# Stores on SyncE's queue, the running state in fp32 beside its block-diagonal copy, and another order in the opening and in block 1

## The chip, the cores and the metric

The kernel runs on one NeuronCore of a Trainium2 chip. The core has five engines that work through their own instruction lists in order and meet only at semaphores: TensorE (PE) multiplies matrices, VectorE (DVE) works element by element, ScalarE (ACT) applies functions and copies, GpSimd (POOL) works element by element and issues DMAs that convert types, and SyncE (SP) issues DMAs. ScalarE can issue DMAs as well. The metric is the device time of one execution in microseconds. A profile of one execution gives the span from the first instruction to the last, and every instruction's place in it.

## The reference: what is computed

A retention layer without softmax, for a batch of 4, 8 heads, 768 steps and a head size of 64, and behind it a two-layer product with a leaky rectifier:

```python
gamma = 1.0 - 2.0 ** (-5.0 - np.arange(H))
for t in range(S):
    state = gamma * state + einsum('bhd,bhe->bhde', k[:, :, t], v[:, :, t])
    y[:, :, t] = scale * einsum('bhd,bhde->bhe', q[:, :, t], state)
x = y.transpose(0, 2, 1, 3).reshape(3072, 512)
h = x @ w_in                                   # 512 -> 2048
g = np.maximum(h, 0) + alpha * np.minimum(h, 0)
out = g @ w_out                                # 2048 -> 512, fp32
```

Inputs and output are fp32.

## The kernel before

**Tiling.** The 3072 steps are cut into 12 units of 256 steps (three per batch element), a unit into two chunks of 128. Two units make a block of 512 tokens; there are six blocks. Within a chunk the retention is a masked product of scores with v; from chunk to chunk a state of 64x64 per head is carried.

**One unit.** `load` (L114) brings q, k and v from SP's queue into four rotating buffers each. `rescale` (L142) multiplies q and k by their decay into the fp16 tile `kdq`, on VectorE or GpSimd; `cast_v` (L155) converts v. The transpose of `kdq` into `kq` is made on TensorE for units 0 to 3 (`turn_pe`, L167: four 128x128 transposes into a PSUM tile `trb`, then a copy by ScalarE), and by a DMA transpose on SP's queue for units 4 to 11 (`turn_dma`, L163). `score_mm` (L243) makes the scores of two of four head pairs, `masks` (L262) multiplies them on VectorE by the causal mask. `sum_mm` (L197) makes the sum of k times v of both chunks in PSUM; the last unit of a batch element needs only its first. `state` (L220) adds the carried state (`ss`, L234) and decays it (`tg`, L239). The result is written, per head pair, as two diagonal 64x64 quarters of a 128x128 fp16 tile whose other quarters were set to zero once; six such tiles rotate (`tgbuf`, L98). The next state reads its predecessor out of that tile. `out_mm` (L275) adds the product of q with the state and the product of the masked scores with v, and ScalarE copies the result as `xT` (L311), the transposed input of the block's first product.

**One block's products.** `ffn1` (L319) is a generator: for each of 16 groups of 128 features it makes four products of 128x128 with 128x512 tokens into one PSUM bank (`hps`, L326), then a rectifier on ScalarE (`hm`, L336) and a combination on VectorE (`gt`, L337). With `early=m` the first m groups are made in two halves of 256 tokens, the first halves ahead of the block's second unit. `ffn2` (L356) makes, for four sets of 128 tokens, 16 products with `w_out` (`ops`, L365); ScalarE evicts each set (`os`, L374, six buffers) and gives out its store from its own queue (L378). For block 0 `ffn2` is cut into four parts by features, so that it can begin before all of `w_out` is there. `tick(gen, m)` (L381) emits the next m products of a generator, so that attention work of later units can be put between them.

**What sets the order.** The kernel writes the order of every engine by hand: an engine and a DMA queue work in the order in which the program emits their instructions. Weights come by DMAs that GpSimd issues with conversion to fp16 (`get_wi`, `get_wo`, L389 and L393). `hold` (L103) makes the next load of a unit wait until a given weight piece has landed: the loads of unit 2 wait for the last piece of `w_in` (L448), those of unit 4 for the last piece of `w_out` (L498). PSUM has eight banks; each call is told which ones it uses, and waits until what was in them has been read.

**The stretches that the change touches.** The opening (L398 to L463) prepares units 0 and 1 and runs block 0's first product; `keep` (L91) issues products of a constant tile ahead of the work. L474 to L519 runs block 0's second product with units 2 and 3 between its pieces and begins block 1's first product. The loop at L522 runs blocks 1 to 5: in each, the next block's two units are rescaled on GpSimd and turned by DMA during the first product, and their attention is put between the pieces of the second product. All `state` calls of units 0 to 3 name VectorE; those in the loop name GpSimd for the decay, except the first of each batch element, which is always on VectorE.

Of the kernel before, what the change touches and what calls it, by code (L numbers as in the profile page):

```python
# [18 lines left out]
def kernel(  # L19
# [169 lines left out]
    def rows(x):  # L189
        return slice(64 * x, 64 * x + 64)  # L190
# [4 lines left out]
    sums = {}  # L195
# [24 lines left out]
    def state(u, c, eng):  # L220

        if (u, c) not in sums:
            return
        s = sums.pop((u, c))
        nxt = (u, 1) if c == 0 else (u + 1, 0)
        tg = tgbuf[(2 * u + c) % len(tgbuf)]
        tgs[nxt] = tg
        if u % UPB == 0 and c == 0:
            eng = nc.vector
        else:  # L230
            old = tgs[u, c]
            ss = sbp.tile([128, NP, 64], FP, tag="ss", bufs=3, name=f"ss{u}_{c}")
            for a in range(2):
                nc.vector.tensor_tensor(  # L234
                    out=ss[rows(a)], in0=old[rows(a), :, rows(a)], in1=s[rows(a)], op=ADD
                )
            s = ss
        for a in range(2):
            eng.tensor_tensor(  # L239
                out=tg[rows(a), :, rows(a)], in0=s[rows(a)], in1=dec[rows(a)], op=MULT  # L240
            )
# [33 lines left out]
    def out_mm(u, banks):  # L275
        _, kq, vx = prepped[u]
        ys = [ps(banks[0], "y0"), ps(banks[1], "y1")]
        inter = [(u, c) in tgs for c in range(2)]

# [75 lines left out]

    def ffn2(n, banks, parts=1):  # L356
        gt = gts.pop(n)
        opss = {}
        step = NFT // parts
        for f0 in range(0, NFT, step):  # L360
            for tq in range(4):
                if f0 == 0:
                    opss[tq] = ps(banks[tq % len(banks)], "ops")
                for ft in range(f0, f0 + step):
                    nc.tensor.matmul(  # L365
                        out=opss[tq],
                        lhsT=gt[:, ft, 128 * tq : 128 * tq + 128],
                        rhs=w_out_all[:, ft, :],
                        start=(ft == 0),
                        stop=(ft == NFT - 1),  # L370
                    )
                    if ft == NFT - 1:
                        os_sb = sbp.tile([128, d_model], FP, tag="os", bufs=6, name="os")
                        nc.scalar.activation(  # L374
                            out=os_sb, in_=opss[tq], func=COPY, bias=0.0, scale=1.0
                        )
                        row = TB * n + 128 * tq
                        nc.scalar.dma_start(out=out[row : row + 128, :], in_=os_sb)  # L378
                    yield
# [17 lines left out]

    nc.scalar.dma_start(out=tab, in_=tab_h.ap())  # L398
# [4 lines left out]
    nc.vector.memset(warm, 0.0)  # L403
    nc.vector.memset(spin, 1.0)  # L404
    nc.scalar.activation(out=warm, in_=warm, func=RELU, bias=0.0, scale=-1.0)
    for t in tgbuf:
        nc.vector.memset(t, 0.0)
    V, G, A = nc.vector, nc.gpsimd, nc.scalar
# [15 lines left out]
    nc.vector.tensor_scalar(  # L424
# [3 lines left out]
    keep(4)  # L428
# [3 lines left out]
    cast_v(A, 0, 4, 8)  # L432
# [4 lines left out]
    state(0, 0, V)  # L437
    turn_pe(1, 0, (2, 3))
    state(0, 1, V)
    out_mm(0, (4, 5))  # L440
    rescale(V, 1, 0, 4, 8)
    rescale(G, 1, 1, 4, 8)
    score_mm(1, 0, (6, 7))
# [12 lines left out]
    state(1, 0, V)  # L456
    state(1, 1, V)
# [8 lines left out]
    def early_prep(u, wos):  # L466
        rescale(V, u, 0, 0, 4)
        rescale(G, u, 1, 0, 4)
        rescale(V, u, 0, 4, 8)
        rescale(G, u, 1, 4, 8)  # L470
        cast_v(A, u)
        return get_wo(wos)

    gen = ffn2(0, (0, 1, 2, 3), parts=4)  # L474
    tick(gen, 18)
# [6 lines left out]
    tick(gen, 5)  # L482
    score_mm(2, 0, (6, 7))
    masks(2, 0)
    tick(gen, 3)
    turn_pe(2, 1, (4, 5))
    cast_v(A, 2)
    tick(gen, 6)
    score_mm(2, 1, (6, 7))
    masks(2, 1)  # L490
    sum_mm(2, (4, 5))
    state(2, 0, V)
    state(2, 1, V)
# [7 lines left out]
    tick(gen, 8)  # L501
    out_mm(2, (6, 7))
    turn_pe(3, 0, (4, 5))
    tick(gen, 5)
    score_mm(3, 0, (6, 7))
    masks(3, 0)
    tick(gen, 3)
    turn_pe(3, 1, (4, 5))
    cast_v(A, 3)
    tick(gen, 6)  # L510
    score_mm(3, 1, (6, 7))
    masks(3, 1)
    sum_mm(3, (4, 5))
    state(3, 0, V)
    state(3, 1, V)
    tick(gen)
    gen = ffn1(1, (0, 1, 2, 3, 4, 5), early=4)
    tick(gen, 16)
    out_mm(3, (6, 7))  # L519


    for n in range(1, NBLK):  # L522
# [4 lines left out]
        if more:  # L527
            for u in (u0, u0 + 1):
                tick(gen, 8 if n > 1 else 4)
                rescale(G, u, 0, 0, 8)  # L530
                rescale(G, u, 1, 0, 8)
                turn_dma(u)
                cast_v(G, u)
                if u + 2 < NU:
                    load(u + 2)
        tick(gen)
# [52 lines left out]
```

## Time and profile before

| What | Number |
|---|---|
| three executions | 232.33, 233.16, 234.44 us (median 233.16) |
| the profiled execution | 233.85 us, span 232.0 us |
| busy share of the span: PE, DVE, ACT, POOL | 89%, 55%, 43%, 29% |
| mean granted TensorE clock | 0.953 |
| TensorE busy, 58.45 to 73.30 us | 4.66 of 14.85 us, granted clock 0.66 |
| TensorE busy, 85 to 228 us | 141.90 of 143.00 us, granted clock 1.00 |
| DMA traffic | 34.01 MB, 147 GB/s on average |

The profile shows one execution. In its rows a group of instructions is named by line, engine, operation and tiles, written `out<-in`; behind it stand the number of instructions, their busy time, the mean of one, and the idle time ahead of them with what ended it. The 40 slices show each engine's busy tenths in equal parts of the span. The chain of work that ended last goes back from the last instruction to what released it, and so on. DMA issues show the time on the issuing queue, and apart from that the time from issue to landing. Releasers are inferred from the times of semaphore events.

### The profile page before, as it was taken

To read this page: it belongs to the slowest core of one execution; us is meant where nothing else is said; L and a number is where in the kernel's file an instruction comes from. 1 tells how busy PE (TensorE), PEld (TensorE's weight loads), DVE (VectorE), ACT (ScalarE), POOL (GpSimd) and SP (SyncE) were. 2 spreads that over 40 slices of the span, in tenths; PEclk is the share of its full clock that TensorE was granted. 3 is DMA by queue.
4 is the path that set the end of the run, shared out by engine and by line. 5 is a ranking of instruction groups with operands and counts; after the bars stand their busy time and mean duration, and the time that the engine had idled before them with its cause. 6 is when DMAs were issued, how large, how long until landed. Compare 5 with 4: busy or idle time off the path is not lost.

```text
span 232.0 us, 4867 instructions
## 1 busy us (share of the span) xinstructions
PE 207.5 (89%) x2045; PEld 105.7 (46%) x2045; DVE 128.7 (55%) x211; ACT 100.8 (43%) x168; POOL 67.4 (29%) x67
## 2 busy tenths in 40 slices
PE   7758899989317999999998999999999999999992
PEld 2436444545205545554453554455544555444440
DVE  4597588266400888602978406986068764288000
ACT  2553764534213672334842337723366323666121
POOL 0491015304920003891004970027900150000000
PEclk9985999999955899999999999999999999999998
DMA  6999999949999930269971199902660011100121
GB/s 186 293 185 196 202 286 276 187 89 271 271 247 270 247 87 3 91 144 285 214 175 48 49 237 283 284 15 91 137 138 0 3 45 72 67 0 0 48 86 53
DMA packets 62791, 34.01 MB, mean 147 GB/s; under 512 B 18080, under 2 KB 59696, under 8 KB 62768
## 3 DMA queue, kind: packets, MB, share of 16 engines
q1 hardware_dynamic: 54240, 23.07, 43.6%
q0 software_dynamic: 4752, 4.19, 11.9%
q10 hardware_dynamic: 3776, 6.43, 8.3%
q8 instruction: 16, 0.26, 0.5%
q14 instruction: 7, 0.06, 0.1%
HBM read 27.40 MB, written 6.29 MB: 145 GB/s over the span
## 4 chain that ended last, share of the span: by engine, by line
PE 80%; DMA 7%; DVE 6%; ACT 4%; issue 1%; POOL 1%; ACTq 0%; POOLq 0%
PE hps L326 37%; PE ops L365 31%; DMA kq<-kdq 4%; PE y L298 3%; DMA ks<-in_k_dram 3%; PE kps L94 3%; DVE m L266 2%; PE y L283 2%; DVE tg L239 1%; ACT xT L311 1%; PE sca L253 1%; PE st L208 1%; DVE ss L234 1%; ACT kq L181 1%; PE trb L175 1%
## 5 line engine op out<-in xcount | busy, mean ns | idle before, releaser
L337 DVE SCALAR_TENSOR_TENSOR gt<-hm,oma,hps 128x512 f16<-128x512 f32 x96 | 69.3, 745 | 58.1 <-ACT hm L336 51.1
L326 PE MATMUL hps<-xT,win 128*128 128x512 f16 (+1 forms) x408 | 88.2, 378 | 11.6 <-ACT os L374 8.8
L365 PE MATMUL ops<-wout,gt 128*128 128x512 f16 x384 | 87.3, 379 | 0.0
L336 ACT ACTIVATE hm<-hps 128x512 f32<-128x512 f32 x96 | 56.6, 597 | 27.2 <-PE hps L326 23.7
L326 PEld LDWEIGHTS <-win 128*128 128x128 f16 x408 | 41.2, 101 | 56.8 <-issue 12.6
L365 PEld LDWEIGHTS <-gt 128*128 128x128 f16 x384 | 36.1, 98 | 42.0
L374 ACT ACTIVATE os<-ops 128x512 f32<-128x512 f32 x24 | 14.3, 597 | 64.6 <-PE ops L365 53.4
L239 POOL TENSOR_TENSOR tg<-ss,tab 64x256 f16<-64x256 f32 x22 | 13.4, 610 | 82.4 <-DVE ss L234 81.5
L145 POOL TENSOR_TENSOR kdq<-qs,tab 128x512 f16<-128x512 f32 (+1 forms) x16 | 24.0, 1502 | 26.8 <-DMA qs<-in_q_dram 26.6
L266 DVE TENSOR_TENSOR m<-sca,mi 128x512 f16<-128x512 f32 x24 | 16.6, 690 | 19.8 <-PE scb L253 19.6
L311 ACT ACTIVATE xT<-y 128x512 f16<-128x512 f32 x24 | 16.0, 739 | 20.8 <-PE y L298 20.8
L145 POOL TENSOR_TENSOR kdq<-ks,tab 128x1024 f16<-128x1024 f32 x8 | 15.2, 1902 | 13.1 <-DMA ks<-in_k_dram 12.7
L266 DVE TENSOR_TENSOR m<-scb,mi 128x512 f16<-128x512 f32 x24 | 16.3, 681 | 0.0
L234 DVE TENSOR_TENSOR ss<-tg,st 64x256 f32<-64x256 f16 x32 | 13.3, 416 | 3.6 <-PE st L208 2.4
L181 ACT ACTIVATE kq<-trb 128x512 f16<-128x512 f16 x16 | 8.7, 597 | 12.5 <-PE trb L175 12.5
L253 PE MATMUL sca<-kq 64*64 64x128 f16 x192 | 8.5, 221 | 2.0 <-ACT kq L181 2.0
L283 PE MATMUL y<-kq,tg 128*128 128x128 f16 x80 | 7.5, 233 | 2.1 <-DVE tg L239 1.4
L253 PEld LDWEIGHTS <-kq 64*64 64x64 f16 x384 | 6.7, 108 | 4.6 <-ACT kq L181 3.0
L161 POOL CAST vx<-vs 128x1024 f16<-128x1024 f32 x8 | 8.5, 1061 | 0.7 <-DMA vs<-in_v_dram 0.7
L94 PE MATMUL kps<-spin 128*128 128x512 f16 x20 | 6.7, 490 | 2.2 <-DVE spin L404 1.5
L253 PE MATMUL scb<-kq 64*64 64x128 f16 x192 | 8.5, 222 | 0.0
L283 PEld LDWEIGHTS <-tg 128*128 128x128 f16 x80 | 5.8, 105 | 5.3 <-DVE tg L239 2.0
(25 smaller groups left out, 66.2 us busy)
## 6 DMA issues: line engine op xcount, KB each, us to landing
out_dram<-os ACTq DMA_DIRECT2D x24, 256.0 KB, 2.9
vs<-in_v_dram SPq DMA_DIRECT2D x10, 512.0 KB, 7.8
ks<-in_k_dram SPq DMA_DIRECT2D x8, 512.0 KB, 6.2
qs<-in_q_dram SPq DMA_DIRECT2D x8, 512.0 KB, 7.0
ks<-in_k_dram SPq DMA_DIRECT2D x8, 256.0 KB, 5.5
qs<-in_q_dram SPq DMA_DIRECT2D x8, 256.0 KB, 5.4
wout<-in_moe_w_out_dram POOLq DMA_DIRECT2D x4, 512.0 KB, 10.9
win<-in_moe_w_in_dram POOLq DMA_DIRECT2D x3, 512.0 KB, 9.5
```

What stands on the lines that cost most here:

```text
L145: eng.tensor_tensor(out=kdq[:, t, :, h0:h1, :].rearrange("p r h d -> p h r d"), in0=staged[u]["kq"[t]][:, h0:h1, :].rearrange("p h (r d) - ...
L234: nc.vector.tensor_tensor(out=ss[rows(a)], in0=old[rows(a), :, rows(a)], in1=s[rows(a)], op=ADD)
L239: eng.tensor_tensor(out=tg[rows(a), :, rows(a)], in0=s[rows(a)], in1=dec[rows(a)], op=MULT)
L253: nc.tensor.matmul(out=scs[a][rows(c), at : at + 128], lhsT=kv[rows(a), 0, r, p, rows(c)], rhs=qmove(kq, a, c, p), start=True, stop=True,)
L266: nc.vector.tensor_tensor(out=m2, in0=live[u, hh][a].rearrange("p (r a i) -> p r a i", r=2, a=2), in1=mask.unsqueeze(2).to_broadcast([128, ...
L283: nc.tensor.matmul(out=ys[c][:, 128 * p : 128 * p + 128], lhsT=tgs[u, c][:, p, :], rhs=kq.rearrange("p (t r a) i -> p t r a i", t=2, r=2)[ ...
L311: nc.scalar.activation(out=xT[n][:, :, at : at + 128].rearrange("k a (p r) -> k a r p", r=2), in_=ys[c].rearrange("k (a r p) -> k a r p", ...
L326: nc.tensor.matmul(out=hpss[ft][:, lo:hi], lhsT=w_in_all[:, hp, 128 * ft : 128 * ft + 128], rhs=xT[n][:, hp, lo:hi], start=(hp == 0), stop ...
L336: nc.scalar.activation(out=hm, in_=hps, func=RELU, bias=0.0, scale=-1.0)
L337: nc.vector.scalar_tensor_tensor(out=gt[:, ft, :], in0=hm, scalar=oma_sb[:, ft : ft + 1], in1=hps, op0=MULT, op1=ADD,)
L365: nc.tensor.matmul(out=opss[tq], lhsT=gt[:, ft, 128 * tq : 128 * tq + 128], rhs=w_out_all[:, ft, :], start=(ft == 0), stop=(ft == NFT - 1),)
L374: nc.scalar.activation(out=os_sb, in_=opss[tq], func=COPY, bias=0.0, scale=1.0)
```

## The change

*Stores.* The store of each evicted set is given out on SP's queue instead of ScalarE's.

*State.* The decayed state is made once as a plain fp32 tile (`tf`, 128x256, four buffers), from which the next state is added. VectorE adds over all 128 partitions in one instruction where it had two of 64 partitions. For the first state of a batch element VectorE multiplies; otherwise the engine that the call names does. Two GpSimd copies then put the quarters into the block-diagonal fp16 tile. All calls of units 0 to 3 now name GpSimd.

*Opening.* Three of the six zero fills go to GpSimd. The second `keep(4)` becomes `keep(3)`. Unit 1's turn and first scores come ahead of unit 0's `out_mm`, whose banks change; GpSimd's rescaling of unit 1 comes ahead of the states. The hold for unit 2's loads is put on the fourth of the five `w_in` pieces. Block 0's first product begins with four groups in halves, not two, with other banks.

*Block 0's second product, units 2 and 3.* The numbers of products between the attention steps change; unit 2's sums and state come ahead of its last masks; `cast_v(A, 3)` comes ahead of unit 3's turn. GpSimd's rescaling of units 4 and 5 and their DMA transposes are emitted here, unit 4's ahead of the last ten products of block 0, the transpose of unit 4 and the loads of unit 6 thus ahead of three of block 0's four stores.

*Block 1's first product* is made unit by unit: `ffn1_unit` makes all 16 feature groups for the 256 tokens of one unit, two groups to a bank. That of unit 2 stands between products of block 0's second, ahead of unit 3's attention. In the loop, block 1 starts with its second product.

The diff, cut to its core:

```diff
@@ state
+        t = sbp.tile([128, NP, 64], FP, tag="tf", bufs=4, name=f"tf{u}_{c}")
+        if u % UPB == 0 and c == 0:
+            nc.vector.tensor_tensor(out=t, in0=s, in1=dec, op=MULT)
+        else:
+            ss = sbp.tile([128, NP, 64], FP, tag="ss", bufs=3, name=f"ss{u}_{c}")
+            nc.vector.tensor_tensor(out=ss, in0=run.pop(), in1=s, op=ADD)
+            eng.tensor_tensor(out=t, in0=ss, in1=dec, op=MULT)
+        run[:] = [t]
...
         for a in range(2):
-            eng.tensor_tensor(
-                out=tg[rows(a), :, rows(a)], in0=s[rows(a)], in1=dec[rows(a)], op=MULT
-            )
+            o, i = tg[rows(a), :, rows(a)], t[rows(a)]
+            nc.gpsimd.tensor_copy(out=o, in_=i)
@@ new generator
+    def ffn1_unit(n, ul, banks):
+        if ul == 0:
+            gts[n] = sbp.tile([128, NFT, TB], F16, tag="gt", bufs=2, name=f"gt{n}")
+        gt = gts[n]
+        cols = slice(U * ul, U * ul + U)
+        for f0 in range(0, NFT, 2):
+            hps = ps(banks[f0 // 2 % len(banks)], "hps")
+            for f in range(2):
+                for hp in range(4):
+                    nc.tensor.matmul(
+                        out=hps[:, U * f : U * f + U],
+                        lhsT=w_in_all[:, hp, 128 * (f0 + f) : 128 * (f0 + f) + 128],
+                        rhs=xT[n][:, hp, cols],
+                        start=(hp == 0),
+                        stop=(hp == 3),
+                    )
...
+            hm = sbp.tile([128, TB], FP, tag="hm", bufs=3, name="hm")
+            nc.scalar.activation(out=hm, in_=hps, func=RELU, bias=0.0, scale=-1.0)
+            for f in range(2):
+                nc.vector.scalar_tensor_tensor(
+                    out=gt[:, f0 + f, cols], in0=hm[:, U * f : U * f + U],
...
@@ ffn2
-                        nc.scalar.dma_start(out=out[row : row + 128, :], in_=os_sb)
+                        nc.sync.dma_start(out=out[row : row + 128, :], in_=os_sb)
@@ opening
-    for t in tgbuf:
-        nc.vector.memset(t, 0.0)
+    for i, t in enumerate(tgbuf):
+        (G if i < 3 else V).memset(t, 0.0)
...
     cast_v(A, 0, 0, 4)
-    keep(4)
+    cast_v(A, 0, 4, 8)
+    keep(3)
...
     sum_mm(0, (0, 1))
-    state(0, 0, V)
+    rescale(G, 1, 1, 4, 8)
+    state(0, 0, G)
+    rescale(V, 1, 0, 4, 8)
     turn_pe(1, 0, (2, 3))
-    state(0, 1, V)
-    out_mm(0, (4, 5))
...
+    score_mm(1, 0, (4, 5))
     masks(1, 0)
-    turn_pe(1, 1, (0, 1))
+    turn_pe(1, 1, (2, 3))
     get_wi(4, 8)
-    get_wi(8, 12)
-    held.append(get_wi(12, 16))
+    out_mm(0, (6, 7))
+    state(0, 1, G)
+    score_mm(1, 1, (4, 5))
     cast_v(A, 1, 0, 4)
-    score_mm(1, 1, (4, 5))
     cast_v(A, 1, 4, 8)
     masks(1, 1)
+    held.append(get_wi(8, 12))
+    get_wi(12, 16)
     sum_mm(1, (2, 3))
...
-    gen = ffn1(0, (0, 1, 4, 5, 2, 3), early=2)
-    tick(gen, 8)
-    out_mm(1, (6, 7))
+    gen = ffn1(0, (6, 7, 0, 1, 2, 3), early=4)
+    tick(gen, 16)
+    state(1, 0, G)
+    out_mm(1, (4, 5))
+    state(1, 1, G)
     tick(gen)
@@ block 0's second product
     gen = ffn2(0, (0, 1, 2, 3), parts=4)
-    tick(gen, 18)
+    tick(gen, 10)
...
     score_mm(2, 1, (6, 7))
+    sum_mm(2, (4, 5))
+    state(2, 0, G)
     masks(2, 1)
-    sum_mm(2, (4, 5))
-    state(2, 0, V)
-    state(2, 1, V)
+    tick(gen, 7)
+    out_mm(2, (6, 7))
+    state(2, 1, G)
...
     held.append(get_wo(3))
     load(4)
     load(5)
-    tick(gen, 8)
-    out_mm(2, (6, 7))
+    tick(gen, 4)
+    half = ffn1_unit(1, 0, (4, 5, 6, 7))
+    tick(half)
+    cast_v(A, 3)
+    tick(gen, 3)
     turn_pe(3, 0, (4, 5))
...
     score_mm(3, 1, (6, 7))
+    sum_mm(3, (4, 5))
+    state(3, 0, G)
     masks(3, 1)
-    sum_mm(3, (4, 5))
-    state(3, 0, V)
-    state(3, 1, V)
+    tick(gen, 8)
+    out_mm(3, (6, 7))
+    state(3, 1, G)
+    rescale(G, 4, 0, 0, 8)
+    rescale(G, 4, 1, 0, 8)
+    cast_v(G, 4)
+    turn_dma(4)
+    load(6)
     tick(gen)
-    gen = ffn1(1, (0, 1, 2, 3, 4, 5), early=4)
-    tick(gen, 16)
-    out_mm(3, (6, 7))
+    half = ffn1_unit(1, 1, (4, 5, 0, 1, 6, 7))
+    tick(half, 20)
+    rescale(G, 5, 0, 0, 8)
+    rescale(G, 5, 1, 0, 8)
+    cast_v(G, 5)
+    turn_dma(5)
+    load(7)
+    tick(half)
```

More of the change, by code (lines that the diff above doesn't have):

```diff
@@ L423 @@
     )
-    nc.vector.tensor_scalar(
+    V.tensor_scalar(
         out=oma_sb, in0=aps[:, 0:NFT], scalar1=-1.0, scalar2=1.0, op0=MULT, op1=ADD
@@ L431 @@
     rescale(G, 1, 1, 0, 4)
-    cast_v(A, 0, 4, 8)
     masks(0, 1)
@@ L526 @@
             gen = ffn1(n, (4, 5, 6, 7, 0, 1))
[L527 to L536, printed above, removed]
+            if more:
+                for u in (u0, u0 + 1):
+                    tick(gen, 8)
+                    rescale(G, u, 0, 0, 8)
+                    rescale(G, u, 1, 0, 8)
+                    turn_dma(u)
+                    cast_v(G, u)
+                    if u + 2 < NU:
+                        load(u + 2)
+            tick(gen)
         gen = ffn2(n, (0, 1))
```

56 lines of the change are left out of this document (22 added, 34 removed).

## The prediction, made before the changed kernel ran

> **What bounds the kernel now.** I read the slices first, then the chain of work that ended last, then the timeline of the one stretch where both look odd, and last the waits. The slices:
>
> ```profile
> PE   7758899989317999999998999999999999999992
> PEclk9985999999955899999999999999999999999998
> DMA  6999999949999930269971199902660011100121
> ```
>
> One slice is 5.8 us. From slice 3 on TensorE is at 8 or 9 tenths, except in slices 10 and 11 (58 to 70 us), where it falls to 3 and 1 tenths; the clock is at half in slices 11 and 12. From 85 to 228 us it is busy 141.90 of 143.00 us: nothing is to be had there but by less TensorE work. The chain in order of time tells what fills the hole:
>
> ```profile
> 53.20 6.10 DMA ks<-in_k_dram
> 59.30 9.03 DMA kq<-kdq
> 68.37 0.04 issue
> 68.41 0.34 ACTq L378
> 68.75 0.05 issue
> 68.80 0.60 ACT os L374
> 69.40 0.04 issue
> 69.44 1.01 PE hps L326 x4
> ```
>
> A transpose on SP's queue ends at 68.33, and 0.08 us later ScalarE's queue gives out a store (L378), behind which the next eviction `os` and then TensorE's `hps` stand. The timeline shows that three of the four stores of block 0 do this:
>
> ```profile
> 58.89 0.36 ACTq L378 DMA_DIRECT2D out_dram<-os  x1
> 59.30 0.60 ACT L374 ACTIVATE os<-ops 128x512 f32<-128x512 f32 x1 [2.95 <-DMA vs<-in_v_dram]
> ...
> 62.51 0.34 ACTq L378 DMA_DIRECT2D out_dram<-os  x1
> 62.90 0.60 ACT L374 ACTIVATE os<-ops 128x512 f32<-128x512 f32 x1 [3.01 <-DMA qs<-in_q_dram]
> ...
> 68.41 0.34 ACTq L378 DMA_DIRECT2D out_dram<-os  x1
> 68.80 0.60 ACT L374 ACTIVATE os<-ops 128x512 f32<-128x512 f32 x1 [5.30 <-DMA kq<-kdq]
> ```
>
> Issue plus time to landing on SP's queue gives 58.8 (v of unit 4), 62.5 (q of unit 5) and 68.3 (transpose of unit 4); the stores go at 58.89, 62.51 and 68.41. So a store waits for an older transfer of the other queue, and ScalarE, which works in order, waits with it. The waits sum it up: `PE hps L326 <- ACT os L374` 8.8 us in 3 times, the longest 4.9. In 58.45 to 73.30, 14.85 us, TensorE is busy 4.66 at a mean clock of 0.66, and block 1's first product runs at half clock until about 76.
>
> **The change part by part.** I follow TensorE in absolute times of the profile.
>
> *Stores on SP.* The wait moves to SP's queue, which computes nothing. ScalarE is free, so the stretch above closes. What stands behind a waiting store on SP is transposes and loads; that is priced below. Issue time: 0.34 us on ACT, SP's own loads 0.37 to 2.6; I take 0.4, nearest to the store's own row. The last store's tail (228.2 to 232.0) stays, within 0.1.
>
> The Trainium skill, "DMA: Bandwidth & Descriptors", section "Issuing engines are not separate DMA queues", speaks against a gain: the issuing engine matters only by the little sequencer time. By it this part would be worth at most the 24 x 0.34 us of issue on ScalarE, all off the path; the 8.8 us wait above disagrees, since an in-order engine also inherits the wait ahead of the issue.
>
> *Opening (0 to 37.25).* One warm-up product fewer, 0.25 (L94, four in 1.02). Unit 1's turn and scores come ahead of unit 0's `out_mm`, which now waits for POOL: rescale ends at 14.6 (as before), two copies into `tg` follow, so `out_mm` starts at 15.4 instead of 13.48. POOL's copy 64x256 has no row; below lies a quarter of the 1.06 cast of 128x1024, 0.27, above the multiply of the same shape, 0.61; I take 0.4, nearest to the cast less a fixed part. The three memsets on POOL lie before q arrives at 5.5: nothing. ScalarE's casts of v1 come behind `xT`: 17.8 to 19.0 against 17.75 to 18.9, so `sum_mm(1)` ends at 19.4 to 20.1 (19.38 before). Then 16 half-width products instead of 8 (0.11 each at full clock, 0.23 at the half clock of 15.8 to 22.5): to 21.2 to 23.7. Meanwhile POOL issues weights (0.8 each, four after state (0,1)) until 20.9, then multiplies and copies state (1,0): 22.3. `out_mm(1)` thus ends at 23.3 to 24.9 (22.87 before), `xT` 1.33 later, and 16 halves (1.8) and 12 full features (10.35) remain: end at 36.8 to 38.3, I take 37.4 (before 37.25). Weights hide: the cast-loading queue is still moving older pieces until 18.2 and lands the last w_in piece at 26.9; the thirteenth feature is wanted at 34. Without that cover each late microsecond would cost one.
>
> *Start of block 0's second product.* Its first bank is now that of feature 14, not 12. Vector frees that bank 0.75 after the end of the first product (groups `gt`, 36.35 + 2 x 0.82 = 38.0): +0.8. So it begins at 38.2.
>
> *38.2 until `sum_mm(4)`.* Work: 71 products of 0.2155 = 15.3; block 1's first product unit by unit, 2 x 64 x 0.111 = 14.2 (eight halves took 0.86 from 24.29; as full products 13.8); units 2 and 3: turns 4 x 0.45, scores 4 x 0.35, sums 0.36 + 0.5, `out_mm` 1.03 + 0.85, together 6.0. Sum 35.5. The first product needs on DVE two 128x256 operations per pair; between 0.42 (64x256 rows of L234) and 0.745 (the 512-wide row), I take 0.42, of the same width: 0.84 against 0.89 on TensorE, hidden; at 0.745 it would cost 8 x 0.6 per unit, 9.6 in all. New waits: turn to scores takes 1.62 (41.13 to 42.75) and now has 4 and 5 products beside it, not 5 and 6: 0.3 + 0.1; `sum_mm(2)` for the cast 0.55 (0.25 before); `out_mm(2)` for masks behind the state add 0.25; the unit's product for `xT` 0.55; unit 3's scores 1.05, because ScalarE casts v3 (1.06) before it turns; small ones 0.2. Sum 3.0. So `sum_mm(4)` comes at 38.2 + 38.6 = 76.8, against 88.85: **-12.05**.
>
> *What is late next.* POOL does the states of unit 3 (DVE add at 65.1, POOL multiply 0.61, two copies) before it rescales unit 4: 67.1 to 70.9 (2 x 1.9), where before it followed the loads at 55.5. Block 0's weight piece and with it the loads of units 4 and 5 also come some 7 us later (POOL issues it at 49.7 behind state (2,0) and unit 3's rescaling, before at 42.04), landing by 72, about when POOL has used them up. Transpose 4 goes at 70.95 and lands in 4.7 to 6.2 (those of 99.43 and 132.33): 75.7 to 77.2, wanted at 77.5: hidden. Behind it on SP stand unit 6's loads (4.5, as 101.34 to 105.87) and three stores (1.2); rescaling unit 5 on POOL ends at 75.8, so the queue decides: transpose 5 goes at 78.7. Second transposes landed after 6.9 to 10.6; with loads ahead of it I take 9.2: 87.9 (85.6 to 89.3). `score_mm(5)` wants it 7.6 after `sum_mm(4)` (88.85 to 96.44), at 84.4. **+3.5**, between 1 and 5.
>
> *State in fp32, later blocks.* DVE adds once where it added twice (0.42 less each), POOL multiplies once and copies twice instead of multiplying twice: 1.4 for 1.22. The next add waits for the multiply alone. Only the units of block 3, with four states (118.8 to 137.1), have TensorE wait for them, 0.66 at 127.6 (it waits for the last add to free the sums' bank); the chain gets over 1 us shorter: **-0.66**. Stores ahead of transposes there: the queue is free for transpose 6 at 106.1 instead of 99.43, transpose 7 lands at about 121.3 and is wanted at 128.5: hidden by 7 us.
>
> Sum: 233.85 (span 232.0 and 1.85 around it) - 12.05 + 3.5 - 0.66 = 224.6. The profiled execution is 0.7 above the median of the three runs (233.16), so I forecast **224.0** for the median.
>
> **The rivals.** *Transpose 5 is in time* (its landing nearer 6.9, or POOL and SP quicker than I add): 220.5. For it: the term is the difference of two long chains; against: loads of unit 6 alone, without any store, keep the queue until 77.5, which with 7.8 to 8.9 to land is still past 84.4. *The clock falls in the wait for transpose 5.* After 3.0 us of idle (60.55 to 63.55) the granted clock fell to half at 63.66, and dense work from 73.29 got it back at 76.1. Here 2.8 us at half clock would lose 1.4, with a second such stretch 3: 225.5 to 227. The Trainium skill, "TensorE: Matmul & The Clock Gate", section "What's actually happening", puts the throttle after an idle window of about 3.4 us that runs freely, so whether a 3.5 us gap hits it is chance; the fall after 3.0 us fits no fixed count of idle time. *The change doesn't do what it says*: ScalarE still waits, for something else, and the 8.8 us stay in the sum: 233. Nothing in the new order has ScalarE wait for a transfer but the casts, whose loads are long in; little chance. *Slower: SP's queue holds up every block.* Place: blocks 2 and 3, where transposes stand behind the previous block's last store. Price: each landing later than the 7 us of slack costs its excess once per block; to outweigh 9.2 and a measurable 2.3 it takes 5.8 in both blocks, so a second transpose that lands 22 us after its issue. Against: none in the trace took over 10.6. Time 236.
>
> **How the numbers follow.** Forecast 0.44, clock 0.22, in time 0.20, no effect or an opening and vector pace at their bad ends 0.08, slower 0.06. The range reaches from in time with a good opening (219.5) to the clock's case with a bad opening, transpose 5 at 89.3 and some vector pace: 230.5. About 1% is what a measurement of this kernel tells from no change; below 230.8 is faster: 0.86, within 0.07, slower 0.07.
>
> **What would show it.** Right: no `ACT os <- DMA` waits and a hole in TensorE of 2 to 5 us only ahead of unit 5's scores, at 84 to 88, released by `kq<-kdq`; `sum_mm(4)` at 76 to 78; block 1's first product in two stretches of about 7.1 us each; POOL's rescaling of unit 4 at 66 to 68. Wrong if the 256-wide pieces are paced by DVE, if the opening's end leaves 36.8 to 38.3, or if idle time appears ahead of the scores of units 6 to 11.

## The result, and the profile after

The changed kernel takes 226.31 us (median of 225.29, 225.69, 226.94 and 227.53), the kernel before 233.69 in the four runs beside it: a ratio of 0.969 [0.962, 0.977]. The forecast was 224.0 with a range of 219.5 to 230.5. The profiled execution is the 225.29 one, with a span of 223.5 us against 232.0 before. The other three had spans of 223.9 to 225.8 at mean clocks of 0.966 to 0.977, where this one has 0.981; they left no profile, so the 1.0 between this execution and the median is not placed here. By an estimate from these clocks, 0.966 would fit two more stretches of 3.41 us at half clock (the length seen below; each lowers the mean of 225 us by 0.0076).

The slices of the changed kernel:

```profile
PE   7766798979899995999999999999999999999992
...
PEclk9998899999999999799999999999999999999998
DMA  6999999945696999939992169981190021100111
```

A slice is 5.6 us here. The hole of 3 and 1 tenths at 58 to 70 us is gone, and with it the half clock of slices 11 and 12. One weak slice is left, the sixteenth (83.8 to 89.4 us), and in the one behind it (to 95.0) the clock is at 7 tenths. The chain of work that ended last shows the place (start, duration, what):

```profile
75.96 1.51 PE ops L395 x7
77.47 0.56 PE st L208 x44
...
79.38 0.39 POOL tg L238
79.77 0.04 issue
79.81 0.24 POOL tg L238
80.06 7.23 DMA kq<-kdq
87.29 0.04 issue
87.33 0.24 PE sca L250
```

`sum_mm(4)` starts at 77.47. The transpose of unit 5 is issued at 80.06, lands at 87.29, and unit 5's scores go at once. The chain puts the issue of the transpose down to POOL's copy `tg`, which ended at 80.05. Releasers are inferred, and this one is a coincidence: SP's own queue shows what held the transpose.

```profile
71.45 2.90 SPq L165 DMA_TRANSPOSE kq<-kdq  x1
74.46 0.53 SPq L125 DMA_DIRECT2D ks<-in_k_dram  x1
75.05 0.57 SPq L125 DMA_DIRECT2D qs<-in_q_dram  x1
75.67 1.69 SPq L125 DMA_DIRECT2D vs<-in_v_dram  x1
77.45 2.50 SPq L408 DMA_DIRECT2D out_dram<-os  x3
80.06 5.20 SPq L165 DMA_TRANSPOSE kq<-kdq  x1
```

POOL has `kdq` of unit 5 ready at 76.1. Up to 80 us SP is at the loads of unit 6 and three stores. (The third experiment moves those loads: the transpose then goes at 77.38, before any such copy.) The waits (total, times, longest):

```profile
ACT os L404 <- PE ops L395: 59.7, 21, 6.8
...
PE sca L250 <- DMA kq<-kdq: 2.3, 1, 2.3
```

No wait of ScalarE for a transfer is in the list; before there were three ahead of `os`, of 3.0, 3.0 and 5.3, and one of 2.5 ahead of `hm`. What the new wait does to the clock is read from the windows; `PEclk` is the granted clock, behind the busy times of the engines:

```profile
core 0: us, PE busy (x) PEld busy (x) DVE busy (x) ACT busy (x) POOL busy (x), PEclk, DMA share, GB/s
77.47:85.00 7.53, 7.53 (x146) 4.29 (x145) 3.56 (x8) 1.20 (x2) 5.72 (x10) 1.00 1.21 290
85.00:97.80 12.80, 10.53 (x111) 5.08 (x106) 2.48 (x4) 3.26 (x5) 7.96 (x6) 0.87 0.79 216
97.80:219.00 121.20, 121.20 (x1095) 59.14 (x1094) 66.23 (x98) 55.81 (x92) 31.67 (x40) 1.00 0.45 114
...
88.68:92.09 3.41, 3.41 (x10) 1.22 (x8) 1.60 (x3) 0.00 (x0) 2.32 (x2) 0.50 1.21 297
```

From 88.68 to 92.09 us TensorE is busy without a gap at half the clock; just ahead of it and behind it the clock is 1.00. From unit 5's first scores to block 2's first product it takes 10.47 us (87.33 to 97.80) where before it took 8.58 (96.44 to 105.02): 1.89 more for the same work. Half of 3.41, 1.71, is the clock; the rest is about the 0.17 by which the scores before began ahead of the end of unit 4's `out_mm` (96.27), while here they begin behind a gap.

The whole difference of the spans can be put together from marks of the two traces:

| Stretch | Before | After | Difference |
|---|---|---|---|
| start to `sum_mm(4)` | 88.85 | 77.47 | -11.38 |
| `sum_mm(4)` to unit 5's scores | 7.59 | 9.86 | +2.27 |
| unit 5's scores to block 2's first product | 8.58 | 10.47 | +1.89 |
| block 2's first product to block 3's | 32.13 | 31.29 | -0.84 |
| from there to the last `os` | 90.44 | 90.44 | 0 |
| last `os` to the end | 4.41 | 3.97 | -0.44 |
| span | 232.0 | 223.5 | -8.5 |

### The profile page after: what moved, and what is told of

Its sections match the earlier page's. It is cut to its first block, busy times and chain, and to the rows that moved or that the text cites. A ratio compares the mean times of both kernels' runs of the same rounds, so it can differ in the third digit from the quotient of the medians.

```text
span 223.5 us, 5019 instructions
## 1 busy us (share of the span) xinstructions
PE 205.9 (92%) x2100; PEld 109.7 (49%) x2100; DVE 117.5 (53%) x194; ACT 101.2 (45%) x168; POOL 81.5 (36%) x104
## 4 chain that ended last, share of the span: by engine, by line
PE 80%; DMA 6%; ACT 5%; POOL 4%; SPq 2%; issue 1%; DVE 1%; DVEq 0%; ACTq 0%; POOLq 0%
PE ops L395 34%; PE hps L324 31%; PE hps L364 6%; DMA kq<-kdq 3%; PE y L296 3%; DMA qs<-in_q_dram 2%; PE y L281 2%; SPq L125 2%; PE st L208 2%; ACT xT L309 2%; ACT kq L181 1%; PE sca L250 1%; ACT vx L159 1%; POOL kdq L145 1%; POOL tg L238 1%
## 5 line engine op out<-in xcount | busy, mean ns | idle before, releaser
L395 PE MATMUL ops<-wout,gt 128*128 128x512 f16 x384 | 89.5, 385 | 0.6 <-DVE gt L335 0.6
L335 DVE SCALAR_TENSOR_TENSOR gt<-hm,oma,hps 128x512 f16<-128x512 f32 x80 | 59.3, 747 | 43.4 <-ACT hm L334 35.5
L324 PE MATMUL hps<-xT,win 128*128 128x512 f16 (+1 forms) x336 | 71.1, 373 | 1.4 <-ACT xT L309 1.4
L324 PEld LDWEIGHTS <-win 128*128 128x128 f16 x336 | 33.3, 99 | 37.9 <-issue 1.4
L238 POOL CAST tg<-tf 64x256 f16<-64x256 f32 x40 | 16.2, 405 | 35.7 <-DVE tf L228 33.8
L232 POOL TENSOR_TENSOR tf<-ss,tab 128x256 f32<-128x256 f32 x16 | 9.8, 610 | 42.3 <-DVE ss L231 41.5
L376 DVE SCALAR_TENSOR_TENSOR gt<-hm,oma,hps 128x256 f16<-128x256 f32 x32 | 14.0, 478 | 8.3 <-ACT hm L374 8.2
L364 PE MATMUL hps<-xT,win 128*128 128x256 f16 x128 | 14.3, 273 | 0.4 <-ACT xT L309 0.4
L181 ACT ACTIVATE kq<-trb 128x512 f16<-128x512 f16 x16 | 8.8, 595 | 12.2 <-PE trb L175 12.2
L364 PEld LDWEIGHTS <-win 128*128 128x128 f16 x128 | 12.5, 98 | 2.5 <-issue 0.7
L231 DVE TENSOR_TENSOR ss<-tf,st 128x256 f32<-128x256 f32 x16 | 6.6, 415 | 8.3 <-PE st L208 5.7
```

The costliest lines, as they stand in the source:

```text
L238: nc.gpsimd.tensor_copy(out=o, in_=i)
L324: nc.tensor.matmul(out=hpss[ft][:, lo:hi], lhsT=w_in_all[:, hp, 128 * ft : 128 * ft + 128], rhs=xT[n][:, hp, lo:hi], start=(hp == 0), stop ...
L335: nc.vector.scalar_tensor_tensor(out=gt[:, ft, :], in0=hm, scalar=oma_sb[:, ft : ft + 1], in1=hps, op0=MULT, op1=ADD,)
L364: nc.tensor.matmul(out=hps[:, U * f : U * f + U], lhsT=w_in_all[:, hp, 128 * (f0 + f) : 128 * (f0 + f) + 128], rhs=xT[n][:, hp, cols], sta ...
L376: nc.vector.scalar_tensor_tensor(out=gt[:, f0 + f, cols], in0=hm[:, U * f : U * f + U], scalar=oma_sb[:, f0 + f : f0 + f + 1], in1=hps[:, ...
L395: nc.tensor.matmul(out=opss[tq], lhsT=gt[:, ft, 128 * tq : 128 * tq + 128], rhs=w_out_all[:, ft, :], start=(ft == 0), stop=(ft == NFT - 1),)
```

## The experiments

The theory going in: the time is won by the stores leaving ScalarE's queue; the new order wins next to nothing and loses some 4 us to a late transpose 5 and the clock. The rival: the new order has the gain, or shares in it, and the stores' queue alone would only move the wait. "Before" in the ratios is the kernel before, on the same chip; brackets hold 95% intervals. The medians of the kernel before lie between 232.8 and 233.7 from one such comparison to the next, so a difference of medians between two experiments is uncertain by up to 0.9 us.

**1. The stores alone.** The kernel before, one line changed:

```diff
-                        nc.scalar.dma_start(out=out[row : row + 128, :], in_=os_sb)
+                        nc.sync.dma_start(out=out[row : row + 128, :], in_=os_sb)
```

> The kernel before with one edit: stores on SP's queue. Theory (the hole at 58 to 73 us is ScalarE waiting behind stores, and only the queue of the stores matters for it): no wait of ScalarE for a DMA, block 1's first product runs on from 58.5, unit 4's sums begin at 76 to 77 (88.85 before), transpose 5 lands long ahead of 84, span 219 to 221, so faster than the changed kernel (223.5). Rival (the hole is filled by the new order, with unit 2's part of block 1's first product put into it): TensorE still idles after 58 us for loads, transposes or copies, span 229 or more.

Measured: 221.65 us, ratio 0.953 [0.948, 0.959], 4.7 us less than the whole change (3.8 by the two ratios). SP's queue of this kernel:

```profile
54.40 2.71 SPq L125 DMA_DIRECT2D vs<-in_v_dram  x1
57.21 3.44 SPq L378 DMA_DIRECT2D out_dram<-os  x4
60.75 4.12 SPq L165 DMA_TRANSPOSE kq<-kdq  x1
...
67.93 4.97 SPq L165 DMA_TRANSPOSE kq<-kdq  x1
```

The four stores now cost SP 3.44 us ahead of transpose 4, and nobody waits for it: both transposes are issued long before `sum_mm(4)`, at 77.13, and no wait of ScalarE or TensorE for a transfer is left. From `sum_mm(4)` on this trace has the old distances (16.17 to block 2's first product, then 32.13). Before minus this kernel is 12.2 us of span: 11.7 ahead of `sum_mm(4)`, 0.4 in the tail. The Trainium skill, "DMA: Bandwidth & Descriptors", section "Issuing engines are not separate DMA queues", has the choice of issuing engine save only the usually small time on its sequencer; here it is 12.2 us for 24 x 0.34 us of issue, because the engine that issues also waits ahead of the issue.

What it waits for, the traces name: the semaphore on which each transfer reports its landing. In the kernel before, the queues of SP and ScalarE share eight of these, and a transfer is held until the one that last used its semaphore has landed. The stores of 58.89, 62.51 and 68.41 have the semaphores of unit 4's v, unit 5's q and unit 4's transpose, which land at 58.81, 62.44 and 68.33. In the kernel of this experiment SP's transfers, the stores among them, take the eight in turn behind the opening, and no store finds its semaphore in use: that of the first, at 57.21, had been free since 41.34. So the wait hasn't moved to SP's queue, it is gone. Whether stores on ScalarE's queue with other semaphores would do as well was not tried.

**2. The new order without the stores.** The changed kernel, the stores back on ScalarE's queue (the line above, the other way).

> The changed kernel with the stores back on ScalarE's queue. Theory (in the new order the transfers that block 0's stores wait for have landed before the sets are evicted at 66 to 70, and on SP the three stores only delay transpose 5): ScalarE waits for no DMA by more than 1 us, transpose 5 goes at 77.5 instead of 80.06 and lands by 85, the wait ahead of unit 5's scores is under 0.5 us (2.3 in the changed kernel), the clock stays up, span 219 to 221. Rival (the stores' queue carries the gain in either order): waits of ScalarE for loads and transposes come back with 3 us or more, span 227 or more.

Measured: 225.13 us, ratio 0.967 [0.962, 0.971]: not what was expected, 219 to 221, though not dearer than the changed kernel. Transpose 5 goes earlier without the stores ahead of it (76.53), but it lands only 0.83 earlier, at 86.46, and TensorE still waits 1.5: in every trace of this case SP's transfers land in the order of their issue, and unit 6's v, ahead of it, lands at 83.79. And ScalarE's waits are back, at another place, as its timeline shows at the end of block 1:

```profile
95.32 0.60 ACT L404 ACTIVATE os<-ops 128x512 f32<-128x512 f32 x1 [0.93 <-PE ops L395]
99.22 0.34 ACTq L408 DMA_DIRECT2D out_dram<-os  x1
99.67 2.73 ACT L334 ACTIVATE hm<-hps 128x512 f32<-128x512 f32 x5 [3.75 <-PE hps L324]
```

The store is given out at 99.22, 3.30 after its `os` ended. SP's load of k for unit 8, on the same semaphore, was issued at 92.28 and took 6.86 to land: 99.14. Five rectifiers `hm` then run in one burst and TensorE waits for what follows. The same happens at 131.35. So in the new order block 0's stores are not held up, but those of blocks 1 and 2 are: where such a wait falls depends on which transfer used the store's semaphore last. With the stores on SP's queue no store waits for a landing, neither in the order before (the first experiment) nor in the new one (the changed kernel). The change without the stores wins 8 us against the kernel before, the stores without the rest 11: both take the same hole away (`sum_mm(4)` comes at 77.29 here, at 77.13 in the first), so the two don't add up.

**3. Unit 6's loads behind transpose 5.** The changed kernel, one call moved:

```diff
     turn_dma(4)
-    load(6)
     tick(gen)
...
     turn_dma(5)
+    load(6)
     load(7)
```

> The changed kernel with unit 6's loads emitted behind transpose 5 on SP instead of ahead of it. Theory (the 2.3 us wait at 85 to 87.3 and the half clock at 88.7 to 92.9 both come from transpose 5 going late on a full queue): transpose 5 goes at 76.2, when GpSimd is through, lands by 82, no wait at 85, clock 1.00 to the end, span 219 to 220. Rival (transpose 5 is bound by GpSimd and by its own 7 us, or unit 6's loads turn late in its place): at most 1 us is gained, or the wait comes back at transpose 6 and 7; span 222 or more.

Measured: 221.98 us, ratio 0.953 [0.948, 0.957]. SP's queue:

```profile
72.49 3.20 SPq L165 DMA_TRANSPOSE kq<-kdq  x1
75.78 1.50 SPq L408 DMA_DIRECT2D out_dram<-os  x3
77.38 3.11 SPq L165 DMA_TRANSPOSE kq<-kdq  x1
80.58 0.53 SPq L125 DMA_DIRECT2D ks<-in_k_dram  x1
```

The transpose is issued 2.68 earlier, TensorE doesn't wait for it, and the clock is 1.00 from the opening on. That is 4.3 us less than the changed kernel by the medians, against the 2.27 + 1.89 = 4.16 of the table (the spans of the two profiled executions differ by 3.1, and this one began block 0's second product 1.02 later, which makes 4.1): the late transpose and the clock behind it are the whole loss, and moving unit 6's loads out of its way is enough to end it. The three stores still stand ahead of it here.

**4. Block 1's first product in one piece.** The changed kernel, `ffn1(1, ...)` behind unit 3's `out_mm` in place of the two calls of `ffn1_unit`:

```diff
-    half = ffn1_unit(1, 0, (4, 5, 6, 7))
-    tick(half)
...
-    half = ffn1_unit(1, 1, (4, 5, 0, 1, 6, 7))
+    half = ffn1(1, (4, 5, 0, 1, 6, 7))
```

> The changed kernel with block 1's first product made over 512 tokens in one piece behind unit 3's out_mm, instead of unit by unit. Theory (the piece ahead of unit 3 pushes GpSimd's rescaling of units 4 and 5 back by 7 us, and the 256-wide products cost 0.3 us more): GpSimd rescales unit 4 at 61 to 63, transpose 5 lands by 83, no wait for it, span 219.5 to 221. Rival (the piece ahead of unit 3 covers copies and masks that TensorE would wait for): the gain at transpose 5 is paid back by waits between 50 and 66 us, span 223 or more.

Measured: 222.55 us, ratio 0.956 [0.950, 0.961]. From block 0's second product to `sum_mm(4)` it is 38.99 us (38.95 to 77.94), in the changed kernel 38.92: making the product unit by unit neither wins nor loses time by itself. Transpose 4 is issued at 67.99 here and transpose 5 at 77.54, in time, though unit 6's loads stand ahead of it as in the changed kernel: GpSimd begins to rescale unit 4 at 61.66, 6 us earlier than there, as was expected. So the late transpose 5 needs both, the late rescaling behind the piece ahead of unit 3 and the loads in the queue; taking either away ends it.

**5. The new order with the old state.** The changed kernel, `state` as before (two additions from the fp16 tile, two multiplies into it, on the engine that the call names).

> The changed kernel with the state of before: two 64-row adds that read the fp16 block-diagonal tile, and the decay written straight into it. Theory (the fp32 state is worth what the four-state chain of units 6 and 7 made TensorE wait, 0.66 to 0.84 us, and one VectorE add of 0.42 in each of two spots of block 0): the wait of 0.7 ahead of unit 6's out_mm comes back, unit 2's and unit 3's steps each lose up to 0.4, the rest is as in the changed kernel; span 224.3 to 225.3 (223.5 in the changed kernel). Rival (the extra GpSimd copies cost as much as the add saves, since GpSimd's chain up to transpose 5 gets shorter without them): transpose 5 goes earlier by 0.4 or more, span 223.5 or less.

Measured: 228.29 us, ratio 0.979 [0.972, 0.985], above what was expected. Two of its waits:

```profile
PE sca L253 <- DMA kq<-kdq: 3.5, 1, 3.5
...
PE y L284 <- DVE ss L234: 0.7, 1, 0.7
```

The stretch of units 6 and 7 is 32.14 us again (31.29 in the changed kernel), with the wait for `ss` that the kernel before has too: the state in fp32 is worth 0.85 there. The rest of this execution's loss is transpose 5: it was issued at 79.88, about as in the changed kernel, and took 8.41 to land instead of 7.23, which makes the wait 3.5 instead of 2.3. The half clock follows in both, here from 88.82 to 92.23. Whether the old state has a part in the longer landing isn't shown. Nor is the median explained: the profiled execution, at 227.05, is the fastest of the four and had no half clock in its opening.

**6. Transpose 5 first, and other banks.** The third kernel, and block 0's second product begins with banks 2 and 3, whose features are read earlier:

```diff
-    gen = ffn2(0, (0, 1, 2, 3), parts=4)
+    gen = ffn2(0, (2, 3, 0, 1), parts=4)
```

> Unit 6's loads behind transpose 5, as in the run before, and besides block 0's second product on banks 2, 3, 0, 1 instead of 0 to 3, so that its first sets do not take the banks of the last two feature groups. Theory (the 1.3 us between the end of the first and the start of the second product is the bank, read last by VectorE): the second product follows the first within 0.1 us; the next thing late is VectorE's rescaling of unit 2 ahead of its transposes, some 0.5 us; net gain 0.8, span 218.3 to 219.7 with a usual opening. Rival (that wait only hides the later one for unit 2's rescaling or for its loads): the same start of unit 2's transposes as in the run before, no gain, the wait moves there.

Measured: 221.79 us, ratio 0.951 [0.946, 0.956], no different from the third's 221.98. The piece itself behaves: the wait of 0.60 ahead of `ops` is gone (the first product's rest takes 27.27 to 39.54, 12.27, where it was 12.87 with the wait), and from the start of that stretch to the end this execution is 0.66 shorter. But that stretch began at 27.27 instead of 26.70, and the total doesn't tell the two apart.

**7. The stores alone, and the fp32 state for block 3's units onward.** The first kernel, with the changed `state` from unit 6 on:

```diff
+        if u >= 2 * UPB:
+            t = sbp.tile([128, NP, 64], FP, tag="tf", bufs=4, name=f"tf{u}_{c}")
...
+            return
```

> The kernel before with stores on SP's queue and the fp32 state from unit 6 on only; opening, order and state of units 0 to 5 as before. Theory (of the new state only the four-state chain of units 6 and 7 is on the path): 0.8 us less than with the stores alone, span 218.6 to 219.4. Rival (that wait is hidden behind something else by then): span 219.8 as with the stores alone.

Measured: **220.58 us**, ratio 0.946 [0.941, 0.952], the least of all that was run, and faster than both kernels. The stretch of units 6 and 7 takes 31.29 (93.06 to 124.35) against 32.13 in the first: -0.84, and the medians differ by 1.07. The two parts that pay are thus the stores (or, by the second experiment, the new order in their place) and the fp32 state where TensorE waits for a chain of four states.

**8. The clock by itself.** The changed kernel, with ten products of the constant tile ahead of unit 5's scores; their result is read by nobody:

```diff
+            if n == 1:
+                keep(10)
             score_mm(u0 + 1, 0, (4, 5))
```

> The changed kernel with ten constant products (2.2 us at full clock, results unused) put in front of unit 5's scores, where TensorE waits for transpose 5. Theory (the wait itself costs 2.3 us and the half clock that follows it, 88.7 to 92.9, another 1.9): transpose 5 lands as before at 87.3, the wait behind the ten products is under 0.5 us, the clock stays at 1.00 from 85 to 95, span 221.4 to 222.0. Rival (the clock falls for another reason, or the products push the scores back by as much): half clock again, or scores after 88.5; span 223 or more.

Measured: 224.98 us, ratio 0.964 [0.959, 0.970], 1.3 less than the changed kernel though its profiled execution left the opening 0.93 later. Its windows, to be compared with the same one of the changed kernel above (0.87):

```profile
85.00:97.80 12.80, 12.32 (x157) 6.39 (x155) 2.48 (x4) 4.12 (x7) 8.90 (x6) 1.00 0.90 221
```

Transpose 5 lands as late as before (80.97 + 7.72 = 88.69), but from unit 5's scores to block 2's first product it now takes 8.77 us (88.74 to 97.51) instead of 10.47. So 1.70 of the 1.89 is the clock, and that is half of the 3.41 us; filling the gap with useless products gets it back, and only an earlier transpose gets the 2.27. The scores lie behind the rival's 88.5, but not because of the products, which end at 88.26: 0.93 is the later opening and 0.49 the longer landing.

**9. The new opening with the old middle.** The seventh kernel, with the fp32 state for all units and the opening of the changed kernel. Its core:

```diff
-    state(1, 0, V)
-    state(1, 1, V)
...
-    gen = ffn1(0, (0, 1, 4, 5, 2, 3), early=2)
-    tick(gen, 8)
-    out_mm(1, (6, 7))
+    gen = ffn1(0, (6, 7, 0, 1, 2, 3), early=4)
+    tick(gen, 16)
+    state(1, 0, G)
+    out_mm(1, (4, 5))
+    state(1, 1, G)
```

> Stores on SP's queue, the fp32 state in all units and the new opening, but units 2 and 3 and block 1's first product in the order of before. Theory (the new opening ends later: GpSimd's copies ahead of out_mm, twice as many half-width products ahead of unit 1's out_mm, and the bank of the second product): the second product begins 0.8 to 1.4 us later than with the old opening (37.4 to 38.2 in the three profiles with it), span 219.6 to 220.6 against 218.8. Rival (the later starts seen with the new opening, 38.4 to 39.6, are only where the clock's half-speed stretch falls): the start lies within 37.4 to 38.2 plus the bank's 0.7, span 219.3 or less.

Measured: 224.94 us, ratio 0.966 [0.962, 0.970]: 4.4 dearer than the seventh, and well above the 219.6 to 220.6 expected. The chain of this trace shows a wait that no other kernel has at this size:

```profile
50.50 0.76 POOL tg L238
51.26 0.08 issue
51.34 1.99 POOL kdq L145 x2
53.33 5.71 DMA wout<-in_moe_w_out_dram
59.05 0.04 issue
59.09 1.46 PE ops L362 x6
```

POOL issues the last piece of `w_out` behind its copies of unit 2's state, which are new there, and unit 3's rescaling: at 53.33, where the kernel before issued it at 42.04. TensorE waits 2.83 us for it. Of the 4.3 by which this span is longer than the seventh's, another 0.77 is a wait for POOL's copies of unit 2's state (1.09 ahead of `out_mm(2)`, against 0.32 for VectorE's there), and 0.77 the opening (the second product starts at 38.71, there at 37.94). In the changed kernel the piece is issued almost as late (50.98), but the products of `ffn1_unit` (51.03 to 58.18) stand ahead of its use. In the fourth, which has no such products there, 0.3 us of the same wait shows. The state's copies on POOL and the unit's product in the middle belong together: one makes the weight late, the other covers it.

**10. The new middle with the old opening.** The third kernel with the opening before, and with the old state for units 0 to 2.

> The opening of before (with its state in units 0 to 2), and behind it the changed kernel with unit 6's loads behind transpose 5. Against the stores alone with the fp32 state late (span 218.8) it differs in the order of units 2 and 3 and of block 1's first product alone. Theory (that order costs TensorE nothing and gains nothing once transpose 5 goes in time, since its waits are only exchanged): span 218.6 to 219.6. Rival (the unit-by-unit product is worth its 2 us of filled waits, hidden so far by the opening): span 218.3 or less.

Measured: 220.78 us, ratio 0.949 [0.943, 0.955]. From the start of block 0's second product to `sum_mm(4)` 38.57 (38.94 in the seventh; 38.93 in the third, which has the same order here), no wait for transpose 5. It equals the seventh kernel (220.58) within the spread of both: with transpose 5 in time, the new order of units 2 to 5 is worth nothing that these runs can tell, over the old one with its stores on SP.

**What the openings say.** Block 0's second product begins, over the profiled executions:

| Opening | Start of the second product, us |
|---|---|
| before's order (before; 1, 7, 10) | 37.41; 38.19, 37.94, 38.90 |
| new order (after; 2, 3, 4, 8, 9) | 38.55; 38.37, 39.57, 38.95, 39.48, 38.71 |
| new order, old state (5) | 38.05 |
| new order, other banks (6) | 39.54 |

Means of 38.1 and 38.9 for the first two rows: the new opening is no gain, and by this rather a loss of 0.8, 0.6 of it the wait for the bank. But one order varies by 1.5 between executions. They differ in the half clock of the first 26 us: it lasts 6.83 us in the four of the first row and in 2, 3, 4 and 8, but 3.41 in the changed kernel and 9, none in 5 and 10.24 in 6. The four of the second row with 6.83 have a mean of 39.1, so like with like the loss is 1.0; one execution of each kernel doesn't settle more.

## Why the prediction came out as it did

The time lies in the range, 2.3 above the forecast, and what was named as signs of being right is there: no wait of `os` for a transfer, a hole of 2 to 5 us only ahead of unit 5's scores, `sum_mm(4)` between 76 and 78, two stretches of about 7.1, unit 4's rescaling between 66 and 68. That the sum's 224.6 comes so near the profiled execution's 225.29 is in part luck: hole, transpose, clock, state and tail miss by +0.67, -1.23, +1.89, -0.18 and -0.44, and these cancel to +0.7. And the 0.6 taken off for the median went the wrong way, since the median lies 1.0 above the profiled execution. By the sum's own terms:

- **The hole closes: right.** -12.05 was forecast, -11.38 measured. `sum_mm(4)` was to come at 76.8 and came at 77.47. The difference lies ahead of 38.2, the forecast start of the second product: it began at 38.55; and in the stretch behind it, 38.92 instead of 38.6 (its terms add to 38.5). The first experiment shows that the stores alone make this term (`sum_mm(4)` at 77.13), the second that the rest of the change alone makes it too (77.29); the third and the tenth show that the two together add nothing measurable.
- **Why it closes: half right.** "The wait moves to SP's queue" is not what happened. ScalarE was held by semaphores that its stores shared with older transfers; on SP's queue the stores find theirs free, and what they cost there is only their place in the queue.
- **The opening: the size was right, the parts were shifted.** Its end was put at 36.8 to 38.3, 37.4 most likely, and it came at 37.95 (25.68 + 12.27). `out_mm(1)` was to end at 23.3 to 24.9; it ended at about 24.3, and `xT` 1.4 later, so the rest of the first product started at 25.68. The wait for the bank, +0.8, was 0.60.
- **VectorE's 256-wide operations: right in effect.** The 0.42 taken from the 64x256 rows was 0.478, within its bounds of 0.42 and 0.745; the pair is 0.956, more than TensorE's 0.89, but TensorE has no wait for it in the list, and the two unit stretches took 7.15 and 6.99 where 7.1 was forecast. GpSimd's copies cost 405 ns, forecast 0.4:

```profile
L238 POOL CAST tg<-tf 64x256 f16<-64x256 f32 x40 | 16.2, 405 | 35.7 <-DVE tf L228 33.8
...
L376 DVE SCALAR_TENSOR_TENSOR gt<-hm,oma,hps 128x256 f16<-128x256 f32 x32 | 14.0, 478 | 8.3 <-ACT hm L374 8.2
```

- **Transpose 5 late: the mechanism was right, the size too large.** +3.5 was forecast, between 1 and 5; it was 2.27. POOL's rescaling of unit 4 was forecast at 67.1 and began at 67.67; transpose 4 at 70.95, it went at 71.45; unit 6's loads and three stores then held SP as forecast, but 8.61 from one issue to the other, not 7.75 (transpose 4's own issue 3.0, the loads 3.0 where 4.5 was taken, the stores 2.6 where 1.2 was), so that transpose 5 went at 80.06 instead of 78.7. It then landed in 7.23, not 9.2, which was taken from the second transposes before (6.9 to 10.6). That landing time is the term that was mis-sized; the fifth experiment measured 8.41 for the same transfer. That unit 6's loads alone would make it late, as the rival's answer had it, is what the second experiment shows.
- **The clock: the forecast's own case was not the one that came.** It left the clock out of the sum and gave the fall to a rival, at 225.5 to 227; that rival happened, with 226.31. Its price, 1.4 for 2.8 us at half clock, measured 1.71 for 3.41 us, and 1.70 by the eighth experiment. The step that failed is the choice between the two cases: with a wait of 3.5 us in the sum and a fall after 3.0 us in the trace of before, the fall was the likelier one. The edges in the trace of before were read too coarsely: the clock is at half from 63.31 to 76.96, 13.65 us, and not from 63.66 to 76.1; 13.65 is four times 3.41.
- **The fp32 state in block 3: right.** -0.66 forecast, -0.84 or -0.85 measured three times over (changed kernel, and experiments 5 and 7).
- **The tail: off.** 0 within 0.1 was forecast for the last store; it took 0.44 less from SP's queue (3.97 against 4.41 from the last `os` to the end). What in it is shorter was not tried.
- **The rivals.** "No effect" and "slower" are out: ScalarE waits for no transfer, and from 97.8 to 219 us TensorE is busy in every microsecond, as the windows above show; the stores on SP do put later transposes back, but not past their use (transpose 6 goes at 98.89, behind block 1's last store at 98.46, and lands at 103.29; unit 6's scores come at 113.6). "Transpose 5 in time" is what the third experiment makes, 221.98, near that rival's 220.5.

What the prediction didn't see is that its one large term can be had by one line of the diff. It priced the change as a sum, and nothing in it asked what that line would be worth without the rest: 4.7 us more than the whole.

## What to carry to other kernels

Put stores on a queue whose engine computes nothing when that queue has slack; an engine in order pays for the wait ahead of an issue, and no row with the issue's 0.34 us shows it. Ask what that wait is for: here it was a completion semaphore shared with an older transfer of another queue, and nothing that the store needed. When that is done, read the queue for what stands ahead of a transfer that someone will soon want: unit 6's loads, wanted much later, cost 4.2 us by standing ahead of transpose 5, whose data had come late too. And price a wait on TensorE together with the clock behind it.

## What the runs showed of the hardware that was not expected

In these traces the granted clock has two values, 1.00 and 0.50, and changes on a grid of 3.413 us. In the changed kernel it changes at 6.76, 20.41, 23.82, 88.68 and 92.09 us: 4, 1, 19 and 1 steps of that length. A gap of 2.27 us in TensorE's work (85.06 to 87.33) was enough for the fall at 88.68, 1.35 us after work had begun again, and one of 3.48 in the fifth experiment for the fall at 88.82; each cost one step of 3.41 at half clock. A longer gap in the ninth, 2.83 us (56.26 to 59.09), left the clock at 1.00, and so did one of 1.47 in the second. The grid tells them apart: the gap of 2.27 leaves 2.06 us idle in one step (85.27 to 88.68), while the step that ends at 58.12 (11 steps behind that trace's last fall, at 20.57) cuts that of 2.83 into 1.86 and 0.97. Two traces don't make a threshold, but the length of a gap alone doesn't decide.

The Trainium skill, "TensorE: Matmul & The Clock Gate", section "What's actually happening", has a window of about 3.4 us that runs freely, and a fall after an idle one. The grid agrees with the window; the step ahead of the fall at 88.68 was busy for 1.35 of its 3.41 us, so it need not be idle throughout.

The same transpose, on the same queue, took 7.23, 7.72 and 8.41 us to land in three traces with the same transfers about it. It landed 1.86, 1.85 and 2.51 us behind the store ahead of it, so part of the spread is the queue's and not its own. Where a wait of 2.27 us is the difference of two long chains, a spread of 1.2 is half of it.
